# Ending the filler products, which hold a bank of a shared PSUM pool, with the first product run (one core)

## The chip, the cores and the metric

One core of one Trainium2 chip. The metric is device time in microseconds (us), the median of several executions; the kernel before takes 215.7 us by this measure. TensorE is called PE in the profile, ScalarE ACT, VectorE DVE, GpSimd POOL, SyncE SP. The span of a profile (213.7 us before) is some 2 us shorter than the time.

## The reference, cut to what matters

A retention layer (a linear recurrence with one decay per head) over q, k, v of shape 4 x 8 x 768 x 64, followed by a normalization and a two-layer ReLU network with a residual.

```python
for t in range(S):
    state = gamma * state + einsum('bhd,bhe->bhde', k[:, :, t], v[:, :, t])
    y[:, :, t] = scale * einsum('bhd,bhde->bhe', q[:, :, t], state)
...
xn = (x - mu) / sqrt(var + 1e-06) * g_ln
out = x + maximum(xn @ w_ch1, 0.0) @ w_ch2        # 512 -> 2048 -> 512
```

The kernel works on 24 tiles of 128 positions. Per tile it transposes k and q (tiles 0 to 6 on TensorE, the later ones by DMA), scales q ("trq"), multiplies q with k ("pa"), masks ("asb"), multiplies with v and the state ("py"), normalizes ("xn", "xnt"), and then runs the "first product" with w_ch1 (L589), a ReLU (L602 on ScalarE or L604 on VectorE), and the "second product" with w_ch2 (L626).

## The kernel before

The order on every engine is fixed when the kernel is built, by a small planner (`plan.order()`) with its own clock in ns. Where the planner sees TensorE idle, `fill` puts in products on zeros (what they are for is in the prediction, under (3)):

```python
def fill(self, out, eng, begin, end, ns, emit):
    done, last = [], begin
    for t in out:
        if t["eng"] == eng and t["start"] < end:
            n = int((t["start"] - last - 60) / ns(last))
            if n > 0:
                done.append({"eng": eng, "emit": lambda eng, n=n: emit(n)})
            last = t["end"]
        done.append(t)
    return done
...
def warm(n):                                  # a filler of n x 128 columns
    if ("mm", "warm") not in held:
        take("mm", "warm", [P, GMAX * P], FP32)
    for w in [GMAX * P] * (n // GMAX) + [P] * (n % GMAX):
        nc.tensor.matmul(held["mm", "warm"][:, 0:w], lhsT=zeros[:, 0:P], rhs=zeros[:, 0:w],
                         start=True, stop=True)          # L650
```

The tile "warm" is taken once and used until the last filler. It comes from the pool "mm", which has two PSUM banks (PSUM is the memory that this kernel's products are written to; one run's result, 128x512 f32, fills one bank), and in which the runs of the first product live too:

```python
("tp", 2, ps), ("pa", 1, ps), ("py", 1, ps), ("pd", 1, ps), ("mm", 2, ps),
...
def e_m1(eng, ...):                           # one run: 16 matmuls into one bank
    p = take("mm", key, [P, two, n * P], FP32)
    for j in range(two):
        for ko in range(KO):
            nc.tensor.matmul(p[:, j, :], lhsT=w1[:, ko, ...], rhs=held["xnt", hb][...],
                             start=(ko == 0), stop=(ko == KO - 1))      # L589
def e_re(eng, ...):                           # empties the bank
    nc.scalar.activation(out=dst, in_=held["mm", key], func=AF.Relu)    # or VectorE
```

All other PSUM is in use (tp 2 banks, pa 2, py 1, pd 1, mm 2: the eight). Loads are issued by GpSimd in this order (a load "lands" when its data has arrived):

```python
first = ["iota", "pos", "k1", "q1", "v1", "w1_0", "k2", "q2", "w1_1", "v2", "k3", "q3", "v3",
         "w1_2", "k4", "q4", "v4", "w1_3", "k5", "q5", "v5"]
```

## Time and profile before

| what | value | from |
|---|---|---|
| time | 215.68 us (215.56 to 215.99) | 3 runs |
| span | 213.7 us | profile |
| TensorE busy | 204.9 us, 96% | page |
| DMA | 90% or more in 24 of 40 slices, up to 134 us | page |

The page's groups (line, engine, operation, out<-in, shapes, count, then busy us, mean ns, and idle time before with its releaser) of the first product and of the fillers:

```profile
L589 PE MATMUL mm<-xnt,w 128*128 128x128 bf16 (+2 forms) x896 | 93.7, 257 | 0.9 <-ACT h L602 0.9
L650 PE MATMUL mm<-zeros 128*128 128x128 bf16 (+1 forms) x34 | 7.9, 362 | 1.5 <-DVE zeros L221 1.2
```

The first product is the largest group, and only 0.9 us of idle time stands before it. The idle column undercounts: ends of matmuls are modelled and reach past the start of the next one. From start to start, a run of 16 takes 0.89 us. The chain that ended last:

```profile
PE 92%; DMA 3%; DVE 1%; issue 1%; POOL 1%; ACT 1%; POOLq 0%; DVEq 0%
```

That is TensorE nearly all the way. Two rows of VectorE belong to the argument, the ReLU that it does for the fourth run of the first product, and the scaling of q behind it:

```profile
20.59 0.69 DVE L604 TENSOR_SCALAR h<-mm 128x512 bf16<-128x512 f32 x1 [1.54 <-PE mm L589]
21.20 0.41 DVE L416 TENSOR_TENSOR trq<-tp,qsc 128x512 bf16<-128x512 bf16 x1
```

### The profile page before, as it was taken

The numbers are of one execution on the slowest core, as the hardware profiler recorded it, in microseconds if no ns is written. First come the engines' busy times: TensorE is split into PE (matmuls) and PEld (weight loads), VectorE is DVE, ScalarE is ACT, GpSimd is POOL, SyncE is SP. The second block draws the span as 40 slices with busy tenths as digits, with TensorE's granted clock in tenths as the row PEclk, the third lists the DMA queues.
The fourth block names the chain that finished last, engine by engine and source line by source line (L and its number), as shares of the span: only waits on it lengthen the run. The fifth ranks groups of instructions, "written<-read, shape, count | busy, mean of one in ns | idle before, by whom it ended". The sixth has DMA issues, their size and how long they took to land.

```text
span 213.7 us, 4698 instructions
## 1 busy us (share of the span) xinstructions
PE 204.9 (96%) x1945; PEld 132.3 (62%) x1966; DVE 121.3 (57%) x235; ACT 80.9 (38%) x152; POOL 89.5 (42%) x105
## 2 busy tenths in 40 slices
PE   7788999999999999999999999999999999999994
PEld 2557999996466456777877785454444444444442
DVE  7685878970745989987872878893511111012121
ACT  5445655673042202645654253145740044430000
POOL 8988789926498296764933830000000000000000
PEclk9999999999999999999999999999999999999999
DMA  7999999999999999999999999720121111011212
GB/s 140 180 179 180 181 157 189 172 184 156 130 203 191 135 243 183 141 171 127 178 140 140 127 176 163 196 81 0 27 71 52 49 49 49 0 52 49 98 49 98
DMA packets 109382, 27.17 MB, mean 127 GB/s; under 512 B 102065, under 2 KB 106417, under 8 KB 109362
## 3 DMA queue, kind: packets, MB, share of 16 engines
q0 software_dynamic: 75984, 13.24, 90.2%
q1 hardware_dynamic: 32194, 13.31, 34.4%
q10 hardware_dynamic: 1184, 0.33, 0.7%
q8 instruction: 15, 0.25, 0.5%
q14 instruction: 5, 0.04, 0.1%
HBM read 27.27 MB, written 6.29 MB: 157 GB/s over the span
## 4 chain that ended last, share of the span: by engine, by line
PE 92%; DMA 3%; DVE 1%; issue 1%; POOL 1%; ACT 1%; POOLq 0%; DVEq 0%
PE mm L589 40%; PE tp L626 39%; PE pa L443 3%; DMA qsb<-in_q_dram 3%; PE py L466 3%; PE pd L512 2%; PE py L462 2%; PE tp L542 1%; PE tp L411 1%; ACT h L602 1%; PE mm L650 1%; POOL k L342 0%; PE tp L403 0%; PE mm L295 0%; DVE xn L475 0%
## 5 line engine op out<-in xcount | busy, mean ns | idle before, releaser
L589 PE MATMUL mm<-xnt,w 128*128 128x128 bf16 (+2 forms) x896 | 93.7, 257 | 0.9 <-ACT h L602 0.9
L626 PE MATMUL tp<-w,h 128*128 128x512 bf16 (+2 forms) x381 | 86.7, 370 | 1.2 <-issue 0.3
L602 ACT ACTIVATE h<-mm 128x512 bf16<-128x512 f32 x88 | 52.5, 597 | 71.0 <-PE mm L589 60.1
L589 PEld LDWEIGHTS <-w 128*128 128x128 bf16 x896 | 65.8, 98 | 19.6 <-issue 1.1
L626 PEld LDWEIGHTS <-h 128*128 128x128 bf16 x400 | 37.3, 98 | 38.8
L634 DVE SCALAR_TENSOR_TENSOR osb<-tp,rstd,x_all 128x512 f32<-128x512 f32 (+2 forms) x25 | 18.2, 728 | 57.3 <-PE tp L626 57.1
L450 DVE TENSOR_TENSOR asb<-pa,mask 128x1024 bf16<-128x1024 f32 x24 | 29.3, 1220 | 9.6 <-PE pa L443 9.5
L480 DVE BATCH_NORM_STATS2 bns<-py 128x6 f32<-128x512 f32 x24 | 16.7, 696 | 14.7 <-PE py L466 14.5
L499 POOL TENSOR_TENSOR vg<-vsb,vsc 128x512 bf16<-128x512 bf16 x16 | 16.9, 1057 | 12.7 <-DMA vsb<-in_v_dram 11.7
L486 ACT CAST x_all<-py 128x512 bf16<-128x512 f32 x24 | 14.0, 584 | 19.1 <-DVE xn L475 19.0
L342 POOL DMA_DIRECT2D qk<-in_k_dram x17 | 15.2, 893 | 14.3 <-DMA tr<-qk 10.7
L342 POOL DMA_DIRECT2D vsb<-in_v_dram x20 | 18.5, 923 | 1.2 <-DMA v<-in_v_dram 0.7
L475 DVE SCALAR_TENSOR_TENSOR xn<-py,mv,gb 128x512 bf16<-128x512 f32 x24 | 18.0, 751 | 0.9
L526 DVE TENSOR_TENSOR state<-pd,gch 64x256 bf16<-64x256 f32 x40 | 16.7, 417 | 0.3
L342 POOL DMA_DIRECT2D qk<-in_q_dram x17 | 15.2, 894 | 2.7 <-DMA w<-in_moe_w_ch_dram 2.7
L650 PE MATMUL mm<-zeros 128*128 128x128 bf16 (+1 forms) x34 | 7.9, 362 | 1.5 <-DVE zeros L221 1.2
L433 DVE TENSOR_TENSOR trq<-tr,qsc 128x512 bf16<-128x512 bf16 x17 | 7.9, 465 | 0.9 <-DMA tr<-qk 0.8
L564 ACT ACTIVATE rstd<-mv,epsb 128x1 f32<-128x1 f32 (+2 forms) x14 | 3.7, 289 | 11.8 <-DVE mv L481 11.8
L466 PEld LDWEIGHTS <-asb 128*128 128x128 bf16 x192 | 7.9, 98 | 0.3 <-DVE trq L416 0.3
L462 PEld LDWEIGHTS <-trq 128*128 128x128 bf16 x80 | 6.0, 98 | 3.2
L466 PE MATMUL py<-vsb,asb 128*128 128x64 bf16 x160 | 7.9, 193 | 0.0
L462 PE MATMUL py<-state,trq 128*128 128x128 bf16 x80 | 7.7, 219 | 0.1
(65 smaller groups left out, 109.3 us busy)
## 6 DMA issues: line engine op xcount, KB each, us to landing
out_dram<-osb SPq DMA_DIRECT2D x23, 256.0 KB, 3.3
w<-in_moe_w_ch_dram POOLq DMA_DIRECT2D x8, 512.0 KB, 10.5
vsb<-in_v_dram POOLq DMA_DIRECT2D x20, 128.0 KB, 8.7
qk<-in_k_dram POOLq DMA_DIRECT2D x17, 128.0 KB, 9.1
qk<-in_q_dram POOLq DMA_DIRECT2D x17, 128.0 KB, 9.7
qsb<-in_q_dram POOLq DMA_DIRECT2D x6, 128.0 KB, 8.9
k<-in_k_dram POOLq DMA_DIRECT2D x3, 128.0 KB, 7.4
v<-in_v_dram POOLq DMA_DIRECT2D x3, 128.0 KB, 9.0
```

The costliest lines, as they stand in the source:

```text
L342: nc.gpsimd.dma_start(out=tile_of(kind, j), in_=src)
L450: nc.vector.tensor_tensor(out=take("asb", t, [P, NPAIR, 2, P], BF16).rearrange("p i a t -> p a i t"), in0=held["pa", t], in1=mask.rearrang ...
L462: nc.tensor.matmul(py[:, 2 * i:2 * i + 2, :], lhsT=held["trq", t][:, i, :], rhs=held["pb", t][:, i, :], start=(mi == 0), stop=False)
L466: nc.tensor.matmul(py[:, h, :], lhsT=held["asb", t][:, h // 2, h % 2, :], rhs=tile_of("v", t)[:, h, :], start=(mi == 0), stop=(mi == n - 1))
L475: nc.vector.scalar_tensor_tensor(out=take("xn", t, [P, DM], BF16), in0=held["py", t].rearrange("p h d -> p (h d)"), scalar=mv[:, t, 0:1], ...
L480: nc.vector.bn_stats(out=bns[:, t, :], in_=held["py", t].rearrange("p h d -> p (h d)"))
L499: e.tensor_tensor(out=take("vg", j, [P, H, D], BF16), in0=tile_of("v", j), in1=vsc[:, cc, :].unsqueeze(2).to_broadcast([P, H, D]), op=ALU. ...
L526: nc.vector.tensor_tensor(out=held["pb", n][o, :, o], in0=held["pd", b][o, :, o], in1=gch[o, cc, :].unsqueeze(2).to_broadcast([D, NPAIR, D ...
L589: nc.tensor.matmul(p[:, j, :], lhsT=w1[:, ko, (ho + j) * P:(ho + j + 1) * P], rhs=held["xnt", hb][:, h0:h0 + n, ko, :], start=(ko == 0), s ...
L602: nc.scalar.activation(out=dst, in_=src, func=AF.Relu)
L626: nc.tensor.matmul(held[key], lhsT=held["h1", hb][:, ho, i * P:(i + 1) * P], rhs=w2[:, ho, cols], start=(ho == 0), stop=(ho == HO - 1))
L634: nc.vector.scalar_tensor_tensor(out=take("osb", key, [P, w], FP32), in0=held[key], scalar=rstd[:, t:t + 1], in1=x_all[:, t, cols], op0=AL ...
```

## The change

Intent: let the fillers end with the first run of the first product, so that their bank is free from the second run on.

```diff
     with tc.manual_schedule():
-        for t in plan.fill(plan.order(), PE, 1100, 20000, lambda at: 110 if at < 11500 else 80, warm):
+        for t in plan.fill(plan.order(), PE, 1100, 14000, lambda at: 110 if at < 11500 else 80, warm):
             t["emit"](t["eng"])
```

In the instruction streams exactly 11 filler matmuls go, in three groups (five, three, three); every engine's order is otherwise the same. The page shows 34 fillers before and 24 after because some matmul records are missing from a trace; the weight loads of L650, 36 and 25, show the 11.

## The prediction

> **What bounds the kernel now.** I read the page first, then the list of TensorE's waits, then the timelines of TensorE, ScalarE, VectorE and GpSimd over the first 50 us, and last the times from issue to landing of single loads. The page:
>
> ```profile
> PE 204.9 (96%) x1945; PEld 132.3 (62%) x1966; DVE 121.3 (57%) x235; ACT 80.9 (38%) x152; POOL 89.5 (42%) x105
> PE   7788999999999999999999999999999999999994
> DMA  7999999999999999999999999720121111011212
> ```
>
> TensorE is busy for 96% of the span, and all that it lacks lies in the first four slices of 5.3 us. DMA is full for the first 26 slices. So two things can set the pace: TensorE's own stream, and loads that come late. TensorE's waits, over the whole span and then from 24 us on:
>
> ```profile
> PE mm L589 <- ACT h L602: 0.9, 2, 0.5
> PE tp L411 <- DMA qsb<-in_q_dram: 0.3, 1, 0.3
> ```
>
> ```profile
> PE tp L626 <- issue: 0.3, 2, 0.2
> ```
>
> The columns are total us, times, longest. The product that the change speaks of (L589) waited twice for the ReLU on ScalarE, 0.9 us together; after 24 us TensorE waits for no other engine and no load at all. What is won before 24 us is therefore kept to the end, if nothing new stops TensorE on the way. TensorE's timeline (start, length in us; ends are modelled, so I use start to start):
>
> ```profile
> 15.85 0.33 PE L650 MATMUL mm<-zeros 128*128 128x128 bf16 x3
> 16.02 1.06 PE L589 MATMUL mm<-xnt,w 128*128 128x128 bf16 x16
> 16.91 0.40 PE L466 MATMUL py<-v,asb 128*128 128x64 bf16 x8
> 17.76 1.05 PE L589 MATMUL mm<-xnt,w 128*128 128x128 bf16 x16 [0.45 <-ACT h L602]
> 18.65 0.39 PE L403 MATMUL tp<-idn,k 128*128 128x128 bf16 x4
> 19.50 1.05 PE L589 MATMUL mm<-xnt,w 128*128 128x128 bf16 x16 [0.46 <-ACT h L602]
> 20.39 0.39 PE L411 MATMUL tp<-idn,qsb 128*128 128x128 bf16 x4
> 20.61 0.33 PE L650 MATMUL mm<-zeros 128*128 128x128 bf16 x3
> ...
> 21.67 0.40 PE L443 MATMUL pa<-trq,trk 64*128 64x128 bf16 x8 [0.28 <-DVE trq L416]
> 22.00 1.96 PE L589 MATMUL mm<-xnt,w 128*128 128x128 bf16 x32
> ...
> 24.03 0.39 PE L403 MATMUL tp<-idn,ksb 128*128 128x128 bf16 x4
> ```
>
> The reader should see that from 16 to 20 us a run of 16 products starts only after ScalarE has emptied the run before, and that the first time two runs follow each other directly (x32) is at 22.00, right after the last filler (L650). The filler's tile is taken once from "mm", a pool of two PSUM banks, and is held until its last use; until then all real products share the other bank. ScalarE's rows show the same turn-taking:
>
> ```profile
> 14.66 0.60 ACT L602 ACTIVATE h<-mm 128x512 bf16<-128x512 f32 x1 [0.94 <-PE mm L589]
> 17.11 0.60 ACT L602 ACTIVATE h<-mm 128x512 bf16<-128x512 f32 x1 [0.44 <-PE mm L589]
> 18.85 0.60 ACT L602 ACTIVATE h<-mm 128x512 bf16<-128x512 f32 x1 [1.14 <-PE mm L589]
> ```
>
> 17.11 + 0.60 = 17.71, product at 17.76; 18.85 + 0.60 = 19.45, product at 19.50. The loads that come next in TensorE's order, with KB and us from issue to landing, and the start of their issues on GpSimd:
>
> ```profile
> ksb<-in_k_dram POOLq DMA_DIRECT2D x1, 128.0 KB, 10.8
> qsb<-in_q_dram POOLq DMA_DIRECT2D x1, 128.0 KB, 10.8
> ```
>
> ```profile
> 12.59 0.89 POOL L342 DMA_DIRECT2D ksb<-in_k_dram  x1 [0.20 <-issue]
> ...
> 19.10 0.89 POOL L342 DMA_DIRECT2D qsb<-in_q_dram  x1 [0.23 <-issue]
> ```
>
> So the k of tile 4 lands at 12.59 + 10.8 = 23.4 and is transposed at 24.03; the q of tile 5 lands at 19.10 + 10.8 = 29.9 and is transposed at 30.51. Both are only some 0.6 us early.
>
> **What the Trainium skill says.** (1) "PSUM — Partial Sum Buffer", section "The four PSUM rules": one matmul output is at most one bank, 512 fp32 columns. A run here (128x512 f32) is one bank, and the trace agrees that a run waits for the reader of its bank. (2) The same page, "Engine vs sequencer instructions": matmuls start and complete in program order. So a product waiting at 17.76 holds up all behind it, and a late load will too. (3) "TensorE: Matmul & The Clock Gate", "What's actually happening": the array's clock is halved by default and after an idle window of about 3.4 us, and released after as long a busy one. This is what the fillers are for. The trace agrees with the start: 11 fillers of 512 columns take 4.24 us from 1.20, and the same filler later takes half as long per start. (4) "Perfetto Trace Analysis", "Optimization Strategy": the same gap repeating on the engine that should be saturated can mean too little PSUM for the next tile. That is the gap at 17.76 and 19.50.
>
> **The change part by part.** The end of filling moves from 20000 to 14000 on the kernel's own planning clock. That clock is no measured time; I use it only for which fillers go. The planner of the unchanged kernel puts the q transposition of tile 2 at 12880 (the filler before it, at 12.59 in the trace, stays), the first run of the first product at 13350, and the tasks after the later fillers at 15630, 16230 and 19850. So three groups go: those at 15.11, 15.85 and 20.61. Nothing is added and no order changes.
>
> - Filler time. The group at 15.11 ends while TensorE waits for VectorE's xn (14.81 + 0.75 = 15.56, next transposition 15.62): worth 0. The other two take 16.02 - 15.85 = 0.17 and 20.78 - 20.61 = 0.17: 0.34 in all.
> - Bank waits. After the run at 16.02 (0.89 start to start) and py (0.23) TensorE could go on at 17.14 instead of 17.76: 0.62. After 17.76 + 0.89 and the k transposition (0.22), at 18.87 instead of 19.50: 0.63. With the second bank free both go: run 2 has the bank that the fillers leave, run 3 the one ScalarE empties at 15.26, run 4 that of run 2.
> - The pa at 21.67 waits 0.28 for VectorE's trq (21.20 + 0.41), which is behind the ReLU at 20.59 on VectorE. That ReLU moves with its product, so part of this wait stays.
>
> Step by step: xn transposition 15.62, run 2 at 15.85 (end 16.74), py 16.75 (its asb ends at 15.48 + 1.21 = 16.69), run 3 at 16.98, k transposition 17.87 (landed at 8.43 + 9.1 = 17.5), run 4 at 18.09. That is 1.41 earlier than 19.50. VectorE's ReLU then comes at 19.18, trq at 19.79, pa at 20.26 and the double run at 20.59 instead of 22.00: 1.4 us won at this point. It would reach the k transposition of tile 4 at 24.03 - 1.41 = 22.62.
>
> But that k lands at 23.4. At the one place where TensorE waited for such a load, it started 0.05 after the landing (2.43 + 6.2 = 8.6, start 8.64). So it starts at 23.45: 0.58 kept, 0.83 given back as a new wait. Next, the q of tile 5 (landed 29.94 with the finer digits, start 29.99 instead of 30.51) allows 0.52. The vg of tile 5 (30.99 + 1.06 = 32.05 on GpSimd, used at 32.74) allows some 0.6; the other loads I went through up to 50 us allow 0.7 or more (the last piece of the second weights lands at 47.9 and is used at 48.8). From 54 us on, the transposed pairs land 3 us or more ahead of their products. Sum: 1.4 won, 0.9 lost to landings, **0.5 us left**. 215.68 - 0.5 = **215.2 us**, 0.24% less.
>
> **The rivals.**
> 1. The whole 1.4 us stays: 214.3. It needs k of tile 4 to land before 22.6. For: nothing in the profile shows TensorE waiting on DMA after 8.64. Against: its issue at 12.59 and its 10.8 us depend on nothing that the change moves (GpSimd's queue there waits for other loads), and DMA is already full.
> 2. Nothing stays: 215.7. The loads may land some tenths later in other runs, and what is early by 0.5 may be early by 0.1; or, in the DMA-full stretch to 135 us, a transposed pair or a weight comes to be the wait. Against: in this trace the slack there is 2 us or more for most.
> 3. Slower: with fewer fillers the clock falls back. For: idle stretches grow to 0.74 us (14.88 to 15.62) and 0.83 us (22.6 to 23.45). Against: the kernel before had a 0.73 us wait at 12.11 without losing the clock, and these are far below the 3.4 us of the skill's page. If it did happen, each 3.4 us at half rate would cost about 1.7 us (my estimate from that page): some 217.
> 4. VectorE's chain becomes the bound between 19 and 23 us (ReLU, trq, state, asb): I have it at 22.2 for the asb that py of tile 3 needs at 22.4. If it is later by up to 1 us it hides inside the wait for k, and costs nothing.
>
> **Range and chances.** The gate by k and q is a landing time that the change does not touch, so I trust it: 0.2 to 0.8 us of gain is the likely band, 214.9 to 215.5. Runs of the kernel before differ by 0.4 us, and rivals 1 and 2 get about one tenth each. Range 214.6 to 215.7. A gain over 2% would need 4.3 us, three times what all the waits and fillers there hold; a loss over 2% needs a clock fall-back of several windows: half a per cent each.
>
> **What would show it.** Right: the last filler lies at 12.6; no wait of L589 for ScalarE's h before 22 us; double run at about 20.6; a new wait of the tile-4 k transposition for its load, of about 0.8 us, ending near 23.45; then everything on TensorE 0.5 us earlier to the end, DMA's landings of the first 35 us unchanged. Wrong: a waited h at 17 or 19 us would mean the bank is not freed by the fillers' end; a k landing near 22.5 would bring rival 1; a gain of 0.5 at 30 us that is gone at 60 would mean a later load or VectorE sets the pace (rival 2); runs of 16 taking 1.8 us instead of 0.9 after 15 us would be rival 3.

## The result, and the profile after

| kernel | median us | range | runs | ratio | 95% interval |
|---|---|---|---|---|---|
| before | 215.72 | 215.56 to 215.99 | 4 | | |
| changed | 214.73 | 214.53 to 214.87 | 4 | 0.9952 | 0.9935 to 0.9969 |

A ratio here is the mean time of one kernel's fast runs over that of the other's of the same rounds, so it is not quite the ratio of the medians. The changed kernel is faster by half a per cent, within the 2% band. The span went from 213.7 to 213.1 us. The page after:

```profile
PE 203.6 (96%) x1935; PEld 131.4 (62%) x1955; DVE 121.3 (57%) x235; ACT 80.8 (38%) x152; POOL 89.8 (42%) x105
PE 87%; DMA 8%; POOL 2%; issue 1%; DVE 0%; POOLq 0%
L589 PE MATMUL mm<-xnt,w 128*128 128x128 bf16 (+2 forms) x896 | 93.7, 257 | 0.0
```

The idle time before L589 is gone, and DMA has gone from 3% to 8% of the chain that ended last. The longest DMA piece of that chain (start, us, what) is the very load that the prediction named:

```profile
12.66 10.68 DMA ksb<-in_k_dram
```

TensorE's timeline after, over the same stretch:

```profile
15.76 0.40 PE L542 MATMUL tp<-idn,xn 128*128 128x128 bf16 x4 [0.67 <-DVE xn L475]
15.99 1.06 PE L589 MATMUL mm<-xnt,w 128*128 128x128 bf16 x16
16.89 0.41 PE L466 MATMUL py<-v,asb 128*128 128x64 bf16 x8
17.13 1.06 PE L589 MATMUL mm<-xnt,w 128*128 128x128 bf16 x16
18.02 0.39 PE L403 MATMUL tp<-idn,k 128*128 128x128 bf16 x4
18.25 1.06 PE L589 MATMUL mm<-xnt,w 128*128 128x128 bf16 x16
19.14 0.39 PE L411 MATMUL tp<-idn,qsb 128*128 128x128 bf16 x4
...
20.42 0.40 PE L443 MATMUL pa<-trq,trk 64*128 64x128 bf16 x8 [0.44 <-DVE trq L416]
20.75 1.96 PE L589 MATMUL mm<-xnt,w 128*128 128x128 bf16 x32
22.55 0.40 PE L466 MATMUL py<-v,asb 128*128 128x64 bf16 x8
23.39 0.40 PE L403 MATMUL tp<-idn,ksb 128*128 128x128 bf16 x4 [0.44 <-DMA ksb<-in_k_dram]
```

and ScalarE's ReLUs:

```profile
17.08 0.60 ACT L602 ACTIVATE h<-mm 128x512 bf16<-128x512 f32 x1 [0.28 <-PE mm L589]
18.22 0.60 ACT L602 ACTIVATE h<-mm 128x512 bf16<-128x512 f32 x1 [0.55 <-PE mm L589]
```

The reader should compare three places. The run at 17.13 starts beside the ReLU of the run before it (17.08), not after it: two banks are in play. The double run comes at 20.75 in place of 22.00: 1.25 us won. Then the transposition of tile 4's k, at 24.03 before, comes at 23.39: only 0.64 us is left, because py (0.23 us) is done at 22.78 and the k lands at 12.66 + 10.68 = 23.34. From there the lead does not change: the pa of tile 23, near the end of the recurrence, was at 149.22 before, and after it is at

```profile
148.59 0.40 PE L443 MATMUL pa<-trq,tr 64*128 64x128 bf16 x8
```

which is 0.63 us earlier.

### The profile page after: what moved, and what is told of

Same layout as the page of the kernel before. It is cut to its first block, busy times and chain, and to the rows that moved or that the text cites. A ratio compares the mean times of both kernels' runs of the same rounds, so it can differ in the third digit from the quotient of the medians.

```text
span 213.1 us, 4678 instructions
## 1 busy us (share of the span) xinstructions
PE 203.6 (96%) x1935; PEld 131.4 (62%) x1955; DVE 121.3 (57%) x235; ACT 80.8 (38%) x152; POOL 89.8 (42%) x105
## 4 chain that ended last, share of the span: by engine, by line
PE 87%; DMA 8%; POOL 2%; issue 1%; DVE 0%; POOLq 0%
PE tp L626 39%; PE mm L589 37%; DMA ksb<-in_k_dram 5%; DMA w<-in_moe_w_ch_dram 3%; PE pa L443 3%; PE pd L512 2%; PE py L466 2%; PE py L462 2%; PE tp L542 1%; POOL k L342 0%; PE tp L403 0%; POOL qsb L342 0%; POOL v L342 0%; POOL w L350 0%; PE tp L411 0%
## 5 line engine op out<-in xcount | busy, mean ns | idle before, releaser
L589 PE MATMUL mm<-xnt,w 128*128 128x128 bf16 (+2 forms) x896 | 93.7, 257 | 0.0
L589 PEld LDWEIGHTS <-w 128*128 128x128 bf16 x896 | 65.7, 98 | 18.5
L634 DVE SCALAR_TENSOR_TENSOR osb<-tp,rstd,x_all 128x512 f32<-128x512 f32 (+2 forms) x25 | 18.2, 728 | 55.3 <-PE tp L626 55.1
L342 POOL DMA_DIRECT2D vsb<-in_v_dram x20 | 18.5, 923 | 1.2 <-DMA w<-in_moe_w_ch_dram 0.8
L433 DVE TENSOR_TENSOR trq<-tr,qsc 128x512 bf16<-128x512 bf16 x17 | 7.9, 463 | 2.9 <-DMA tr<-qk 2.9
L650 PE MATMUL mm<-zeros 128*128 128x512 bf16 (+1 forms) x24 | 6.4, 394 | 1.4 <-DVE zeros L221 1.2
```

The source lines that it names most:

```text
L342: nc.gpsimd.dma_start(out=tile_of(kind, j), in_=src)
L589: nc.tensor.matmul(p[:, j, :], lhsT=w1[:, ko, (ho + j) * P:(ho + j + 1) * P], rhs=held["xnt", hb][:, h0:h0 + n, ko, :], start=(ko == 0), s ...
L634: nc.vector.scalar_tensor_tensor(out=take("osb", key, [P, w], FP32), in0=held[key], scalar=rstd[:, t:t + 1], in1=x_all[:, t, cols], op0=AL ...
```

## The experiments

Theory: the fillers cost time because they hold a bank, not because of their own work; and of what the free bank wins, late loads take part back. Rivals: the gain is the filler's own time on TensorE; or the landing of loads is not what limits it. In the expectations, "bank theory" is the first half of this theory and "gate theory" the second: a load that TensorE waits for is a gate. All experiments were timed in five rounds, each beside its own runs of the kernel before, and each profile is of one execution. e1 to e4 ran on one chip, e5 to e8 on a second, e9 to e11 on a third and e12 on a fourth, so kernels of different groups are compared by their ratios. Us are medians; the gain is (1 - ratio) times the median before. The intervals are about ±0.0013, which is ±0.28 us.

| label | kernel | us | before | ratio | gain us |
|---|---|---|---|---|---|
| (first result) | changed | 214.73 | 215.72 | 0.9952 | 1.0 |
| e1 | changed, repeated | 215.09 | 215.56 | 0.9977 | 0.5 |
| e2 | one filler left that holds the bank | 215.43 | 215.56 | 0.9995 | 0.1 |
| e3 | only the last fillers removed | 214.79 | 215.56 | 0.9967 | 0.7 |
| e4 | all fillers kept, in another bank | 214.69 | 215.56 | 0.9958 | 0.9 |
| e5 | changed, k of tile 4 later | 215.66 | 215.46 | 1.0003 | -0.1 |
| e6 | before, k of tile 4 later | 215.76 | 215.46 | 1.0002 | 0.0 |
| e7 | changed, k of tile 4 earlier | 214.82 | 215.46 | 0.9959 | 0.9 |
| e8 | before, k of tile 4 earlier | 215.47 | 215.46 | 0.9999 | 0.0 |
| e9 | changed, repeated again | 214.98 | 215.52 | 0.9972 | 0.6 |
| e10 | changed, a run drawn ahead of that k | 214.65 | 215.52 | 0.9957 | 0.9 |
| e11 | changed, three runs drawn ahead | 214.75 | 215.52 | 0.9965 | 0.8 |
| e12 | e10, and one trq moved on VectorE | 214.63 | 215.58 | 0.9956 | 0.9 |

### e1_after_again: the changed kernel once more

```diff
-        for t in plan.fill(plan.order(), PE, 1100, 14000, ...
+        for t in plan.fill(plan.order(), PE, 1100, 13000, ...
```

> Filler end at 13000 in place of 14000: instruction for instruction the changed kernel (no filler lies between), so this is a repeat of it on one chip beside the next three. Bank theory with the load gate: 0.5 to 1.0 us under the kernel before (214.7 to 215.2), and in the profile the double run of products at about 20.7 us and the k transposition of tile 4 waiting for its load until about 23.4 us. If the gain seen first was chance: within 0.2 us of the kernel before.

The instruction streams are identical to the changed kernel's. Gain 0.5 us (0.9977, interval 0.9965 to 0.9990), clear of zero, at the low edge of what was expected. Its profile did not show the wait that was expected, but one like it, a little earlier:

```profile
20.08 0.40 PE L411 MATMUL tp<-idn,qsb 128*128 128x128 bf16 x4 [0.81 <-DMA qsb<-in_q_dram]
...
23.69 0.40 PE L403 MATMUL tp<-idn,ksb 128*128 128x128 bf16 x4
```

Here the q of tile 3, issued at 9.30 as ever, took 10.7 us to land (20.0) in place of 9.2 (18.5), and TensorE waited for it; the double run slipped to 21.37, the k of tile 4 landed at 23.64, and the lead at the pa of 27.48 was 0.33 us in place of 0.63. So in this execution another late load than in the first one set the size of the gain. Of the 14 profiles, nine had this q at 18.2 to 18.6 us and five at 19.6 to 20.1 us; kernels with and without the late fillers are in both groups.

### e2_hold_one: bank held, work gone

```diff
-        for t in plan.fill(plan.order(), PE, 1100, 14000, ...
+        for t in plan.fill(plan.order(), PE, 1100, 20000, ...
-            if n > 0:
+            if (n := min(n, t["start"] > 19500) if t["start"] > 14000 else n) > 0:
```

Ten of the eleven removed matmuls stay removed; a single one of 128 columns stands where the last group stood.

> All fillers after 14000 go as in the change, except one single 128-column product where the last group stood (0.06 us of work), which keeps the bank held to about 20.5 us. Bank theory: run 3 and run 4 of the products still wait for ScalarE, as before, the double run comes at about 21.8 us, and only the 0.34 us of filler is won, of which some is lost to waits: 0.1 to 0.4 us under the kernel before, so 0.3 to 0.7 us over the changed kernel. Rival, filler time: nearly the whole gain stays, within 0.1 us of the changed kernel.

```profile
17.50 1.05 PE L589 MATMUL mm<-xnt,w 128*128 128x128 bf16 x16 [0.44 <-ACT h L602]
...
19.24 1.05 PE L589 MATMUL mm<-xnt,w 128*128 128x128 bf16 x16 [0.46 <-ACT h L602]
...
20.35 0.22 PE L650 MATMUL mm<-zeros 128*128 128x128 bf16 x1
```

One product on zeros brings both waits for ScalarE back, with the 0.44 and 0.46 us of the kernel before, and the gain falls to 0.1 us (0.9995, interval 0.9982 to 1.0007). The filler's own time is not the cause. In this profile it is worth 0.16 us at most: TensorE was 0.10 us ahead of the kernel before at its pa of 14.55, before the first removed filler, and 0.26 us at its pa of 21.67. It kept 0.23 us as far as the pa of 131.42 and had lost it by that of 135.99, behind a trq that took 0.97 us beside GpSimd's vg (e9 tells of this).

### e3_end_19000: only the last three fillers go

```diff
-        for t in plan.fill(plan.order(), PE, 1100, 14000, ...
+        for t in plan.fill(plan.order(), PE, 1100, 19000, ...
```

> Filler end at 19000: only the last group of three short fillers (0.17 us of work) goes, the two groups at 15 and 16 us stay. Bank theory: the bank is free from run 3 on, the double run comes at about 20.8 us, the wait for the load of tile 4 hides the 0.17 us of filler that stays, so the time equals the changed kernel within 0.2 us. Rival, filler time: at most 0.17 us under the kernel before.

Against the kernel before, three matmuls of 128 columns, 0.17 us of work, are gone. The fillers at 15.22 and 15.97 us are still in its timeline, and yet:

```profile
17.27 1.06 PE L589 MATMUL mm<-xnt,w 128*128 128x128 bf16 x16
...
18.38 1.06 PE L589 MATMUL mm<-xnt,w 128*128 128x128 bf16 x16
```

No wait for ScalarE, and a gain of 0.7 us, four times the work removed. What matters is when the bank is given back.

### e4_other_bank: every filler kept

Against the kernel before:

```diff
-        if ("mm", "warm") not in held:
-            take("mm", "warm", [P, GMAX * P], FP32)
+        if ("pd", "warm") not in held:
+            take("pd", "warm", [P, GMAX * P], FP32)
...
-            nc.tensor.matmul(held["mm", "warm"][:, 0:w], ...
+            nc.tensor.matmul(held["pd", "warm"][:, 0:w], ...
```

> All fillers stay to 20000, but they write into the bank that the state products use only from 20 us on, so both banks of the product pool are free all the time. Bank theory: no product run waits for ScalarE, the filler's 0.34 us on the path hides in the wait for the load of tile 4, and the time equals the changed kernel within 0.2 us. Rival, filler time: the time of the kernel before, 215.7.

All fillers stand, and the gain is 0.9 us (0.9958): no less than the changed kernel's. It is 0.4 us under e1, which ran beside it, where at most 0.2 us was expected; e1's profile had a late q of tile 3 (20.0), this one an early one (18.2). The filler group on the path is visible, and so is the wait for the load that swallows it:

```profile
19.18 0.33 PE L650 MATMUL pd<-zeros 128*128 128x128 bf16 x3
...
20.57 1.96 PE L589 MATMUL mm<-xnt,w 128*128 128x128 bf16 x32
...
23.05 0.40 PE L403 MATMUL tp<-idn,ksb 128*128 128x128 bf16 x4 [0.29 <-DMA ksb<-in_k_dram]
```

In this execution k landed at 23.0. With e2 and e3 the first rival has fallen three times: work removed without the bank wins next to nothing, and the bank without the work wins as much as the change.

### e5_q4_first_changed and e6_q4_first_before: the load a little later

The issues of k and q of tile 4 change places on GpSimd; the streams of all other engines are the same instructions in the same order. The same edit on the changed kernel (end 14000) and on the kernel before (end 20000):

```diff
+    todo, i, j = plan.order(), loaded['k', 4], loaded['q', 4]; i, j = todo.index(i), todo.index(j); todo[i], todo[j] = todo[j], todo[i]
     with tc.manual_schedule():
-        for t in plan.fill(plan.order(), PE, ...
+        for t in plan.fill(todo, PE, ...
```

> Changed kernel, with the issues of the k and the q of tile 4 swapped on GpSimd and nothing else, so that this k lands about 0.85 us later (near 24.2 us). Gate theory: the transposition of that k waits until about 24.25 us in place of 23.4, all behind it is 0.85 us later, and nearly all of the gain is gone: 215.4 to 215.8. Rival, the landing is not what limits the gain: no change against the changed kernel, about 214.8.

> The kernel before with the same swap. Gate theory: its transposition was at 24.03 us, so a landing near 24.2 costs it only some 0.2 us: 215.7 to 216.0, and the two kernels with the swap are within 0.3 us of each other. Rival: unchanged 215.7, with the swapped changed kernel still 0.5 to 1.0 us faster.

In the changed kernel:

```profile
22.57 0.40 PE L466 MATMUL py<-v,asb 128*128 128x64 bf16 x8
23.96 0.40 PE L403 MATMUL tp<-idn,ksb 128*128 128x128 bf16 x4 [1.00 <-DMA ksb<-in_k_dram]
```

and in the kernel before:

```profile
23.64 0.40 PE L466 MATMUL py<-v,asb 128*128 128x64 bf16 x8
23.89 0.40 PE L403 MATMUL tp<-idn,ksb 128*128 128x128 bf16 x4
```

The k landed at 23.91 and 23.85, some 0.5 us later than without the swap (0.85 was expected). The two kernels, 1.07 us apart one step earlier (22.57 against 23.64), reach the transposition together, and their times are the same: 1.0003 and 1.0002 of the kernel before. The whole gain is gone by one load that is half a microsecond later. The rival that the landing does not limit the gain has fallen.

### e7_k4_early_changed and e8_k4_early_before: the load earlier

```diff
+    todo, i, j = plan.order(), loaded['w1', 2], loaded['k', 4]; todo.remove(j); todo.insert(todo.index(i), j)
```

> Changed kernel, with the k of tile 4 issued before the third slice of the first weights, and nothing else. That k lands near 21 us and does not gate; the weight slice lands near 23.4 and its first product, which would follow at 23.0, waits for it. Gate theory: 0.1 to 0.4 us faster than the changed kernel, with a wait on the weights in place of the wait on k. Were there no further gate: 0.6 to 0.8 us faster.

> The kernel before with the same earlier k. Nothing there waits for it (used at 24.03, landed 23.4; the weight slice lands near 23.4 and is used at 24.25), so no change: within 0.2 us of the kernel before under both theories. If it gains 0.3 us or more, the order of loads has an effect of its own that the gate theory does not have.

The kernel before did not change (0.9999), as expected. The changed kernel gained 0.9 us, within the spread of its own three series (0.5 to 1.0), so the time tells nothing. The wait for weights that was expected did not come. The profile shows why: k landed at 20.7 and was not waited for, but the execution was one with a late q of tile 3, and the weights slice landed at 23.29, just ahead of its run:

```profile
19.72 0.40 PE L411 MATMUL tp<-idn,qsb 128*128 128x128 bf16 x4 [0.59 <-DMA qsb<-in_q_dram]
...
23.09 0.39 PE L403 MATMUL tp<-idn,ksb 128*128 128x128 bf16 x4
23.33 1.07 PE L589 MATMUL mm<-xnt,w 128*128 128x128 bf16 x16
```

So the loads behind that k leave hardly any room, and in this execution another late load, q, set the pace.

### e9_changed_third: the changed kernel a third time

No edit.

> The changed kernel itself, beside the next two. Gain 0.4 to 1.0 us (the two series so far: about 1.0 and 0.5 us by the ratio of fast runs); in its profile one late load is the wait between 19 and 24 us (k of tile 4, or q of tile 3), and TensorE is 0.3 to 0.7 us ahead of the kernel before from 28 us on.

Gain 0.6 us. The k was waited for again until 23.16 (landed 23.1), and TensorE was 0.85 us ahead at the pa of 27.48 (0.3 to 0.7 was expected). But its lead fell to 0.52 us at the pa of 100.60. TensorE, VectorE and GpSimd there:

```profile
100.08 0.40 PE L443 MATMUL pa<-trq,tr 64*128 64x128 bf16 x8 [0.27 <-DVE trq L433]
```

```profile
93.16 0.41 DVE L433 TENSOR_TENSOR trq<-tr,qsc 128x512 bf16<-128x512 bf16 x1
...
98.86 1.17 DVE L433 TENSOR_TENSOR trq<-tr,qsc 128x512 bf16<-128x512 bf16 x1
```

```profile
98.71 1.04 POOL L499 TENSOR_TENSOR vg<-vsb,vsc 128x512 bf16<-128x512 bf16 x1 [3.43 <-DMA vsb<-in_v_dram]
```

The same trq takes 0.41 us alone and 1.17 us when it starts while GpSimd scales a v. It ends at 100.03, which is 0.28 us after GpSimd's end (98.71 + 1.04 = 99.75). In the kernel before the two met later in GpSimd's instruction (trq at 99.71, vg to 100.19), and trq took 0.75 us, to 100.46: 0.27 after GpSimd's end. The Trainium skill, page "SBUF — State Buffer", section "Who interferes with whom", says that a VectorE instruction with two SBUF inputs contends with a GpSimd instruction that reads SBUF; both inputs of trq lie in SBUF, and the trace agrees, with 0.41 against 0.75 and 1.17 us. The 14 profiles hold a control. Tiles 0 to 6 make trq in another line (L416), from a "tp" that lies in PSUM, so that only one input lies in SBUF. Inside a vg it takes no longer, as in the kernel before:

```profile
25.85 0.41 DVE L416 TENSOR_TENSOR trq<-tp,qsc 128x512 bf16<-128x512 bf16 x1
```

```profile
25.69 1.06 POOL L499 TENSOR_TENSOR vg<-vsb,vsc 128x512 bf16<-128x512 bf16 x1
```

Over all profiles 25 trq of L416 started during a vg, and all took 0.41 or 0.42 us. Of L433, with both inputs in SBUF, 39 did: 38 of them ended 0.27 to 0.33 us after the vg, and the one left had started within 0.01 us of it. GpSimd's start was set by the landing of a v, which did not move as far as TensorE did (vg came 0.44 us earlier than before, TensorE 0.85). So an earlier TensorE can run VectorE deeper into GpSimd's instruction and give back 0.3 us.

### e10_run_before_k4 and e11_three_swaps: filling the landings with work

On the changed kernel, on TensorE alone, the product run behind tile 4's k transposition is drawn ahead of it (e10); in e11 also the runs behind the q transpositions of tiles 4 and 5.

```diff
+    todo, pe = plan.order(), lambda f, **k: ...      # the place of a task in the order
+    (i, j) = (pe('e_tk', t=4), pe('e_m1', key=('1', 0, 8))); todo[i], todo[j] = todo[j], todo[i]
+    # e11 also: e_tq of tile 4 with run ('1', 1, 8), e_tq of tile 5 with run ('1', 1, 12)
```

> Changed kernel, but on TensorE the product run that follows the k transposition of tile 4 goes before it (its weights landed at 22.5 us, the k at 23.3), so that the landing is filled with work. Gate theory: no wait for that k; the next gate is the q of tile 4 (lands 24.1, would be used at 23.9), so another 0.3 us or so over the changed kernel: 214.3 to 214.7. If the landing of k is not what limits: equal to the changed kernel.

> As the run before it, with two more product runs drawn ahead of the transpositions of the q of tile 4 and of tile 5. Gate theory: these landings are filled too, the next gate is the scaled v of tile 4 and tile 5 from GpSimd (ready at about 26.7 and 32.0 us), and TensorE is 1.0 to 1.2 us ahead of the kernel before at 33 us: 0.4 to 0.6 us faster than the changed kernel, 214.1 to 214.6 by time. Rival: later loads or VectorE take it back, and it equals the changed kernel.

```profile
19.64 0.40 PE L411 MATMUL tp<-idn,qsb 128*128 128x128 bf16 x4 [0.57 <-DMA qsb<-in_q_dram]
...
23.00 1.06 PE L589 MATMUL mm<-xnt,w 128*128 128x128 bf16 x16
23.90 0.39 PE L403 MATMUL tp<-idn,ksb 128*128 128x128 bf16 x4
```

That is e10: the wait for k is gone. Both executions profiled were ones with a late q of tile 3 (e11 waited 0.89 us for it), and both lost 0.4 us of their lead between 93 and 101 us, where trq took 1.25 us (e10) and 1.17 and 1.10 us (e11) beside GpSimd's vg. The ratios, 0.9957 and 0.9965, are in the range of the changed kernel's series (0.9952 to 0.9977). e10 is 0.3 us under e9, which ran beside it, as was expected, but the intervals overlap, so that e10 is faster is not shown. For e11 the expected 0.4 to 0.6 us did not come, the rival written beside it did.

### e12_trq_before_stats: the later loss taken away

e10, and on VectorE that one trq goes ahead of the statistics of the tile before, into a stretch in which VectorE waits:

```diff
+    todo.insert(pe('e_bn', t=14), todo.pop(pe('e_eq', t=15)))
```

> The kernel of the run-before-k4 experiment, and on VectorE the one trq of tile 15 (near 99 us, where three of the profiles show it at 1.1 to 1.25 us in place of 0.41, beside GpSimd's vg) goes ahead of the statistics of tile 14, into the 1.3 us in which VectorE waits for py. Theory, that trq waits for GpSimd's vg: it takes 0.42 us there, TensorE's pa at about 100 us has no wait for trq, and the lead that TensorE has at 95 us over the kernel before is kept to the end: 0 to 0.4 us faster than the run-before-k4 kernel, 214.3 to 214.7. Rival, it is slow for another reason: it is still over 0.6 us, or pa still waits.

```profile
95.47 0.41 DVE L433 TENSOR_TENSOR trq<-tr,qsc 128x512 bf16<-128x512 bf16 x1
```

```profile
99.37 0.40 PE L443 MATMUL pa<-trq,tr 64*128 64x128 bf16 x8
```

The trq takes 0.41 us there, and pa does not wait. In this execution (early q of tile 3) TensorE was 1.27 us ahead at the pa of 27.48 and still 1.23 us at the last pa: the span is 212.5 us, the shortest, and that execution took 214.27 us. By the median, 214.63 us (0.9956, interval 0.9942 to 0.9970), it is clearly faster than the kernel before; against the changed kernel's ratios of 0.9952, 0.9977 and 0.9972 it is not shown to be faster. That the loss at 100 us is gone rests on this one profile, and in some of the other profiles (the changed kernel's first one, e1) it did not occur either.

## Why the prediction was right

The time, 214.73 us, lies in the range of 214.6 to 215.7, near its low end; the forecast was 215.2. Two further series put the gain at 0.5 (interval 0.2 to 0.8) and 0.6 us (0.3 to 0.9), the first one at 1.0 (0.7 to 1.4); the forecast was 0.5. The mechanism, a bank that comes free and a late load that takes part of it back, is what the runs show. The closeness of e1's 0.5 to the forecast is in part luck: in the one execution profiled, another load than the forecast one held TensorE. By the prediction's own steps:

- Which fillers go: right. The last one left starts at 12.65 us, and 11 matmuls went.
- The bank waits: right. The waits of L589 for ScalarE, 0.9 us by the page, are 0.0, and e2 brings them back with a single filler. The filler's time was put at 0.34 us on the path; no part of it shows in the final gain, for with all of it left in place e4 gains as much.
- The double run at 20.59: measured at 20.75, in an execution whose pa at 14.55 was already 0.13 us late. The wait of pa for trq, of which part was to stay, grew from 0.28 to 0.44 us: the 0.17 us of the filler at 20.61 became wait, since trq moves with its ReLU. The prediction's step by step had this right, its list of parts not.
- The gate at tile 4's k: right, and the step that carries the number. Forecast 23.45, measured 23.39, 0.05 us after the landing. The wait, from py's end at 22.78, was 0.6 us and not the 0.83 written down, because what came before it was a little later. e5 and e6 confirm it from the other side.
- The second gate, q of tile 5, was to allow only 0.52 us. This term was mis-sized: in the changed kernel's profile that q landed at 29.4 in place of 29.9, and was used at 29.87 without a wait.
- "DMA's landings of the first 35 us unchanged" was the assumption behind trusting the two gates, and it failed. In the changed kernel's profile the issues up to 20 us are within 0.1 us of their old places (some later ones come up to 0.6 us earlier), but landings vary from execution to execution: k of tile 4 landed between 22.9 and 23.7 us in the ten profiles with the old order of issue, and q of tile 3 at 18.2 to 18.6 or at 19.6 to 20.1. The prediction had this only as a rival of one tenth, and did not list the q of tile 3 as a gate: it landed at 18.48 in the profile before, and TensorE 1.4 us earlier would ask for it at 18.98, a slack of 0.5. These landings set the lead in single profiles (0.33 us at the pa of 27.48 in e1, 0.63 in the first result's, 0.85 in e9). Whether they also make the gain 0.5 in one series and 1.0 in another is not shown: one execution of each series was profiled, and the intervals of the series overlap (0.7 to 1.4 against 0.2 to 0.8). Why an execution falls in one group or the other stays open.
- Rival 1 (all of the 1.4 us stays) failed for the changed kernel, for the reason given. e12 comes near it (1.27 us) once the landing is filled with work. Rival 2 holds in part: 0.3 us was given back at about 100 us in some executions, but by GpSimd and VectorE meeting, which the prediction did not see; it looked at the slack of loads alone (and counted 26 full DMA slices where the page has 24, which changes nothing). Of this loss two cases stay unexplained: in e4 a trq at 118.84 took 1.22 us, with only load issues on GpSimd beside most of it, and in e6 one at 66.51 started during a load issue, 0.52 us before the next vg, and took 1.89 us. Rival 3 (the clock) did not occur: runs of 16 took 0.89 us as before the change (0.99 where a pa follows), even after e5's idle stretch of 1.2 us (22.8 to 23.96). The prediction's "11 fillers of 512 columns" at the start are nine of 512 and two of 128 columns, merged in one row; the reading of the clock stands, for those of 512 start 0.43 us apart there and 0.22 us apart from 6.38 us on. Rival 4 did not either: VectorE's asb was done at 22.39, before py at 22.55.

## What to carry to other kernels

Filler work is not free because it is cheap: look at what it holds. A scratch tile taken from a shared pool costs a whole buffer until its last use, so end it early or put it where nothing is needed yet. Before you count a gain in front of a full DMA queue, list the next few loads with their landing and their use: the smallest slack is the gain that survives, and here landings varied by more than half a microsecond from execution to execution. An engine that comes earlier can also run into an instruction of another engine whose start a load has fixed.

## What the Trainium skill lacked or had wrong

- "SBUF — State Buffer", section "Who interferes with whom": agrees in kind; it gives no size for two tensor inputs in SBUF. Here trq took 0.41 us alone and up to 1.25 us when it started during GpSimd's vg, and 38 of 39 such trq ended 0.27 to 0.33 us after that instruction's end: as if they waited for all of it. The section says that a tensor_tensor does not contend with the descriptor generation of GpSimd's loads (inferred there); 91 of the 93 trq of L433 that started during such an issue took 0.41 to 0.43 us, but one in e4 took 1.22 us and one in e6 1.89 us, which is unexplained.
- "DMA: Bandwidth & Descriptors": I found nothing on how much a landing varies. The same 128 KB load, issued at 9.15 to 9.34 us, landed at 18.2 to 18.6 us in nine profiles and at 19.6 to 20.1 us in five.
